# A fused attention and two-layer feed-forward kernel: w_out loaded per unit, y's first tile prepared in wider steps, attention spread evenly

## The chip, the cores and the metric

The program runs on one core of a Trainium2 chip. The metric is the device time of one execution in microseconds; less is better.

## The reference

q, k and v have the shape 4 x 8 x 576 x 64 (batch, heads, positions, columns). Per head there are two attentions: one over positions averaged in groups of four (144 x 144), whose output is repeated four times, and one over a band of seven positions around each query. Their sum, as 2304 tokens of 512 columns, goes through two feed-forward blocks:

```python
out_up = np.repeat(sm_attn(q_d, k_d, v_d), factor, axis=2)
out_local = softmax(where(abs(i - j) < 4, scale * q @ k.T, -1e9)) @ v
x = (out_up + out_local) as (2304, 512)
h = ((x @ w1) * (x @ w2)) @ w3          # 512 -> 1024 -> 1024
y = h @ w_out                           # 1024 -> 512
h2 = y @ w_in                           # 512 -> 2048
out = (h2 * sigmoid(h2)) @ w_out2       # 2048 -> 512
```

The weights arrive as 64-bit floats and are turned into pairs of 32-bit numbers on the chip. Every large matmul is made of three passes (line 31): high times high, low times high, high times low.

## The kernel before, in words

**Opening (about the first 110 us).** The weights w3 and w_out of the first block are loaded, decoded to 32 bits (`decode`, line 140: one activation on ScalarE and four instructions on VectorE, lines 164 to 176, and a split in high and low in lines 188 and 189) and multiplied with each other to one matrix WP (`wprime`, line 438), since nothing stands between them. The first attention steps run beside that.

**Slots.** Then come 192 slots, each a group of 12 matmuls: `ab_group` (line 529, x @ w1 or x @ w2 for one of eight pieces m of 128 columns) and `y_group` (line 570). A token group is a batch b and a part h of 320 or 256 tokens. Batches 0 to 2 go through h = 0 and h = 1 in turn, 16 ab slots each, and the 8 y slots of a group stand behind the first two ab slots of the next one. Batch 1 begins at slot 40, batch 2 at 88, batch 3 at 136. In batch 3 the pieces m < 4 of both parts come first; its last ab slots are 178 to 183 and its last y slots 184 to 191. The accumulators of ab and y have four PSUM buffers (tag mm). The copies `af` (line 545) and `yo` (line 587) on ScalarE and the product `cf` (line 552) on VectorE free them. `yo` has two SBUF buffers, each of which is stored to DRAM (line 589) before it is used again.

**Attention steps.** 48 steps (16 pairs of heads; `scores`, `turn`, `sums`, lines 402 to 417) are put between the slots by a pace: after slot i the steps up to n // 3 + 1 have been written, with n from line 828. `sums` makes x (`make_x`, line 378: the high half on ScalarE, line 392, and the low half on GpSimd, line 393). An ab group needs the x of its four pairs; the last x of batch 1 is made in step 25, of batch 2 in step 37, of batch 3 in step 48.

**Background work.** The weights of the second block, w_in and w_out2, are loaded, decoded and stored to DRAM in 16 units (`bg_steps`, line 632), planned for slots 14 to 166. The weights w12 for m = 4 to 7 are decoded at slots 0, 4, 7 and 10, and used from slots 8, 10, 12 and 14 on. What `at(slot, ...)` plans for a slot is written ahead of it, behind the last instructions marked on ScalarE, VectorE and GpSimd (`behind`, line 812). SP's requests are not held by that.

**Order.** The order of the instructions of each engine, up to the last stage, is set by a scheduler when the program is built: of what is ready it takes what was written first. In the last stage the order of TensorE, VectorE, ScalarE and GpSimd is that of the program (line 966). SP issues every DMA, in an order that the scheduler sets throughout, and waits for each request's buffer before it sends the next.

**First tile of y.** The last stage works on three tiles of 768 tokens. `y_load` (line 737) brings a tile from DRAM into one buffer (tag raw). From its four blocks `y_mix` (line 750, GpSimd) makes four differences t1 to t4, and `y_high` (line 759, ScalarE) and `y_rest` (line 765, GpSimd for even i, VectorE for odd i) split seven blocks into high and low. Later tiles do this inside the units; for tile 0 it is planned behind slot bg_end = 169, with all of it in slots 170 to 174 (lines 803 to 807).

**Last stage, 24 units.** `h_unit` (line 908) makes seven products (a scheme with seven instead of eight block products) of a tile with 256 columns of w_in: for each i six matmuls into one of two PSUM buffers (tag S), then sums on VectorE (line 914); the first product is copied to `p1` on ScalarE (line 932). `silu` (line 889) then makes the two halves of g: a sigmoid on ScalarE, a multiply and a rounding on VectorE (lines 896 and 897) and the low half on GpSimd (line 899); the second half's are put off to the next group by `after`. The 12 `out_block`s (line 845) of unit u, three matmuls each, run between the groups of unit u + 1, two behind each but the first. They need the piece p of w_out2 for that unit: `wo_load(p)` (line 786), 1 MB from DRAM into a buffer with the tag wA (p < 4, taken over from w12) or wC (taken over from WP). The first four are planned for slots 184 to 187, the others are written ahead of unit 0. After the last unit of a tile six outputs of 128 x 512 are copied to SBUF, into three buffers (line 862), and stored in two pieces each (line 869).

Of the kernel before, what the change touches and what calls it, by code (L numbers as in the profile page):

```python
# [8 lines left out]
F32 = mybir.dt.float32  # L9
# [26 lines left out]
def tile_model(ctx: ExitStack, tc: tile.TileContext, qk, vw, vr, w12, w3t, wo, wb, out):  # L36
    nc = tc.nc
# [28 lines left out]
    def s_tile(name):  # L66
        return ps.tile([P, 512], F32, tag="S", name=name, bufs=2)

    ident = cst.tile([P, P], F32, name="ident")
    make_identity(nc, ident)  # L70

# [642 lines left out]
    def at(slot, fn):  # L714
        plan.setdefault(slot, []).append(fn)
# [34 lines left out]
    def y_mix(t, i):  # L750
        b = Y[t]
        out_, in0, in1 = (("t1", "b12", "b11"), ("t2", "b22", "t1"),
                          ("t3", "b22", "b12"), ("t4", "t2", "b21"))[i]
        b[out_] = b["b12"] if i == 2 else yp[0].tile(
            [P, 2, NH], F32, tag=out_, name=f"{out_}_{t}"
        )
        nc.gpsimd.tensor_tensor(out=b[out_], in0=b[in0], in1=b[in1], op=ALU.subtract)
# [4 lines left out]
        nc.scalar.copy(d[:, 0], Y[t][name])  # L762
        YC[t, i] = d

    def y_rest(t, i):
        d = YC[t, i]
        e = nc.vector if i % 2 else nc.gpsimd
        e.tensor_tensor(
            out=d[:, 1], in0=Y[t][CH[i][0]], in1=d[:, 0].bitcast(F32), op=ALU.subtract
        )  # L770
# [29 lines left out]
        y_load(0)  # L800

    at(bg_end, open_y)
    for i in range(4):
        at(bg_end + 1 + i // 2, lambda i=i: y_mix(0, i))
    for i in range(7):
        at(bg_end + 1 + i // 2, lambda i=i: y_high(0, i))
        at(bg_end + 2 + i // 2, lambda i=i: y_rest(0, i))
    at(end_b + 1, lambda: wc_load(0))
    at(end_b + 2, lambda: wc_load(1))
    for p in range(4):  # L810
        at(end_a + 1 + p, lambda p=p: wo_load(p))
    def behind(fns):
        if not fns:
            return
# [6 lines left out]
    for i, slot in enumerate(slots):  # L821
        run_plan(36 + i)
        if i == 13:
            assert n_jobs[0] == len(jobs)
            cpool_b[0] = pool(s_cb, "cpool_b", "right", bufs=2)
        behind(plan.pop(i, []))
        slot()
        n = 36 + max(0, i - 3) if i < 40 else 72 + ((i - 39) * 36) // 46
        run_steps(n // 3 + 1)
        if not opened and done_steps[0] == NSTEP:  # L830
            s_att.close()
            late.append(pool(s_late, "late", "left"))
            opened = True
            assert i < starts[N_EARLY], (i, starts[N_EARLY])
# [4 lines left out]
    s_c.close()  # L839
    s_x.close()  # L840
    b2 = pool(ctx, "b2", "right", bufs=2)
    for p in range(4, 8):
        wo_load(p)

    todo = []

    def out_block(u, half, j):
        t, p = divmod(u, 8)
        if p == 0 and half == 0:
            OUT[t, j] = ps.tile(  # L850
                [P, 512], F32, tag="T" if j < 2 else "mm", name=f"o{t}_{j}",
                bufs=2 if j < 2 else 4,
            )
        acc = OUT[t, j]
        g, w = G[u, half], WO[p]
        for n, (a, b) in enumerate(PASSES):
            nc.tensor.matmul(  # L857
                acc, lhsT=g[:, a, j * P:(j + 1) * P], rhs=w[:, b, half, :],
                start=(p == 0 and half == 0 and n == 0), stop=(p == 7 and half == 1 and n == 2),
            )  # L860
        if p == 7 and half == 1:
            o = b2.tile([P, 512], F32, tag="o", name=f"os{t}_{j}", bufs=3)
            if j % 2:
                nc.vector.tensor_copy(o, acc)
            else:
                nc.scalar.copy(o, acc)
            for k in range(2):
                r0 = 64 * ORDER[(t * 2 * NH + j * P) // 64 + k]
                nc.sync.dma_start(out[r0:r0 + 64, :], o[64 * k:64 * k + 64, :])
# [19 lines left out]
    def silu(u, half, c):  # L889
        sg = temp("sg", f"{u}_{half}", 2, 2 * NH)  # L890
        nc.scalar.activation(sg, c, AF.Sigmoid)  # L891
        g = b2.tile([P, 2, 2 * NH], F32R, tag="g", name=f"g{u}_{half}", bufs=5)
        G[u, half] = g

        def rest():
            nc.vector.tensor_tensor(out=sg, in0=c, in1=sg, op=ALU.mult)
            nc.vector.tensor_copy(g[:, 0], sg)  # L897
            e = nc.vector if u == NUN - 1 else nc.gpsimd
            e.tensor_tensor(  # L899
                out=g[:, 1], in0=sg, in1=g[:, 0].bitcast(F32), op=ALU.subtract  # L900
            )

        if half == 0:
            rest()
        else:
            after(1, rest)

    def h_unit(u):
        t, p = divmod(u, 8)
        wc = WC.pop(u)  # L910
        k = {}

        def tt(out_, in0, in1, op=ALU.add):
            nc.vector.tensor_tensor(out=out_, in0=in0, in1=in1, op=op)  # L914

        cf = temp("c", f"f{u}", 2, 2 * NH)
        cg = None
        for i, (name, w, c) in enumerate(CH):
            acc_full = s_tile(f"h{u}_{i}")
            acc = acc_full[:, :NH]  # L920
            y = YC[t, i]
            n = 0
            for kt in range(2):
                for (a, b) in PASSES:
                    nc.tensor.matmul(  # L925
                        acc, lhsT=wc[w][:, a, c, kt * P:(kt + 1) * P], rhs=y[:, b, kt, :],
                        start=(n == 0), stop=(n == 5),
                    )
                    n += 1
            if i == 0:  # L930
                k["p1"] = temp("p1", u)
                nc.scalar.copy(k["p1"], acc)  # L932
            elif i == 1:
                tt(cf[:, :NH], acc, k["p1"])
            elif i == 2:
                k["u2"] = temp("u2", u)
                tt(k["u2"], acc, k["p1"])
            elif i == 3:
                k["u4"] = temp("u4", u)
                tt(k["u4"], acc, k["u2"])  # L940
            elif i == 4:
                tt(cf[:, NH:], acc, k["u4"])
            elif i == 5:
                cg = temp("c", f"g{u}", 2, 2 * NH)
                k["u3"] = temp("u3", u)
                tt(k["u3"], acc, k["u2"])
                tt(cg[:, NH:], acc, k["u4"])
            else:
                tt(cg[:, :NH], k["u3"], acc, ALU.subtract)
            next_chain()  # L950
            if i == 4:
                silu(u, 0, cf)
            elif i == 6:
                silu(u, 1, cg)
            if p == 7 and t + 1 < NT:
                after(1, lambda i=i: y_high(t + 1, i))
                after(3, lambda i=i: y_rest(t + 1, i))
            if 2 <= p < 6 and i == 5 and t + 1 < NT:
                y_mix(t + 1, p - 2)
            run_out(2 if i else 0)  # L960
        wc_load(u + 2)
        if p == 1 and t + 1 < NT:
            y_load(t + 1)
# [67 lines left out]
```

## Time and profile before

| | us |
|---|---|
| median of 3 runs | 899.86 |
| lowest and highest | 895.21, 900.3 |
| the profiled execution | 895.1 |
| its span, first to last instruction | 893.3 |
| TensorE busy in it | 852.6 |
| mean granted clock of TensorE | 0.987 |

The profile is of one execution, not of the median: durations and waits are read from it and summed against its 895.1 us. A group of rows of one kind gives busy time, the mean of one in ns, and the idle time of the engine ahead of it with what ended that. In a row of the timeline the brackets hold the idle time ahead of the instruction and its releaser.

### The profile page before, as it was taken

Reading aid. Unit: us, or ns where it says so; the run is one execution under the profiler, and the core shown is the slowest. Engines: PE = TensorE matmul, PEld = TensorE weight load, DVE = VectorE, ACT = ScalarE, POOL = GpSimd, SP = SyncE. Lnnn points to the kernel's source line nnn. Section 1 sums busy time; section 2 is a strip of 40 time slices with the busy share of each in tenths; the row PEclk is TensorE's granted clock in tenths of the full one; section 3 lists DMA queues with packets and bytes.
Section 4 is the critical chain, followed back from the end, with each engine's and each line's share of the span. In section 5 each row is a group of like instructions: output and inputs, shape, how many; then the busy total and the mean of one; then the engine's idle time right before and its main releaser. Section 6 shows DMA issues by size and latency. Waiting matters only on the chain.

```text
span 893.3 us, 17448 instructions
## 1 busy us (share of the span) xinstructions
PE 852.6 (95%) x7104; PEld 749.6 (84%) x7104; DVE 532.6 (60%) x852; ACT 300.9 (34%) x865; POOL 286.2 (32%) x224
## 2 busy tenths in 40 slices
PE   3999999998999999999999799999999999999996
PEld 2544598998999899999999788889889898888885
DVE  5999988675575857437954244435644356543434
ACT  5765556354444444433422111113111113211101
POOL 2000144354352534322328022424424236221220
PEclk9999998999999999999999999999999999999999
DMA  9935634554446463406983932424644242542403
GB/s 334 353 106 196 220 133 158 190 181 167 171 159 198 142 225 115 164 27 208 335 344 122 369 124 92 156 83 151 190 142 154 83 154 94 174 145 84 164 2 71
DMA packets 39729, 149.17 MB, mean 167 GB/s; under 512 B 4448, under 2 KB 11616, under 8 KB 33504
## 3 DMA queue, kind: packets, MB, share of 16 engines
q1 hardware_dynamic: 39648, 148.05, 48.0%
q8 instruction: 56, 0.92, 0.4%
q14 instruction: 25, 0.20, 0.1%
HBM read 115.52 MB, written 32.51 MB: 166 GB/s over the span
## 4 chain that ended last, share of the span: by engine, by line
PE 81%; DVE 8%; DMA 4%; ACT 2%; issue 2%; POOL 2%; SPq 1%; POOLq 0%; ACTq 0%; DVEq 0%
PE o L857 21%; PE ab L538 20%; PE h L925 19%; PE y L578 9%; PE wp L448 4%; PE ol L368 2%; PE tl L344 1%; PE sd L276 1%; PE s L325 1%; DMA out<-os 1%; PE od L310 1%; PE td L293 1%; DMA ydram<-yo 1%; DMA st<-w 1%; DMA yr<-ydram 1%
## 5 line engine op out<-in xcount | busy, mean ns | idle before, releaser
L857 PE MATMUL o<-wo,g 128*128 128x512 f32 x864 | 223.8, 395 | 0.0
L857 PEld LDWEIGHTS o<-wo,g 128*128 128x128 f32 x864 | 160.3, 188 | 27.2
L899 POOL TENSOR_TENSOR g<-sg,g 128x768 fp32r<-128x768 f32 x46 | 85.0, 1847 | 260.2 <-DVE g L897 244.6
L925 PE MATMUL h<-yc,wcb 128*128 128x384 f32 x576 | 118.6, 342 | 4.6 <-ACT p L932 4.6
L538 PE MATMUL ab<-x,w_wB 128*128 128x320 f32 (+1 forms) x768 | 114.3, 303 | 3.6 <-POOL x L393 2.1
L925 PEld LDWEIGHTS h<-yc,wcb 128*128 128x128 f32 x576 | 105.2, 190 | 13.7 <-ACT p L932 5.8
L538 PE MATMUL ab<-x,w_wA 128*128 128x320 f32 (+1 forms) x768 | 111.3, 302 | 1.8 <-ACT yo L587 1.8
L538 PEld LDWEIGHTS ab<-x,w_wB 128*128 128x128 f32 x768 | 106.5, 192 | 5.5 <-POOL x L393 2.6
L563 POOL TENSOR_TENSOR c<-cf,c 128x320 fp32r<-128x320 f32 (+1 forms) x64 | 73.2, 1145 | 117.9 <-DVE c L562 109.3
L578 PE MATMUL y<-c,w_wC 128*128 128x320 f32 (+1 forms) x768 | 109.7, 298 | 0.0
L538 PEld LDWEIGHTS ab<-x,w_wA 128*128 128x128 f32 x768 | 105.2, 192 | 3.2 <-ACT yo L587 2.0
L578 PEld LDWEIGHTS y<-c,w_wC 128*128 128x128 f32 x768 | 103.2, 188 | 1.3 <-issue 1.0
L925 PE MATMUL h<-yc,wca 128*128 128x384 f32 x432 | 83.6, 337 | 1.9 <-DVE cg L914 1.9
L891 ACT ACTIVATE sg<-cf 128x768 f32<-128x768 f32 x24 | 20.3, 847 | 184.4 <-DVE cf L914 184.4
L925 PEld LDWEIGHTS h<-yc,wca 128*128 128x128 f32 x432 | 76.8, 188 | 6.2 <-DVE cg L914 2.3
L448 PE MATMUL wp<-w_wo,w_w 128*128 128x512 f32 x128 | 61.3, 622 | 2.6 <-DVE w_w L176 2.6
L552 DVE TENSOR_TENSOR cf<-ab,af 128x320 f32<-128x320 f32 (+1 forms) x64 | 28.9, 452 | 55.5 <-PE ab L538 48.1
L235 POOL TENSOR_TENSOR vr<-vr 72x512 f32<-72x512 f32 x12 | 20.4, 1701 | 102.7 <-PE od L310 84.3
L891 ACT ACTIVATE sg<-cg 128x768 f32<-128x768 f32 x24 | 20.3, 847 | 90.0 <-DVE cg L914 90.0
L914 DVE TENSOR_TENSOR u<-h,u 128x384 f32<-128x384 f32 x48 | 26.6, 554 | 39.8 <-PE h L925 39.6
L249 ACT ACTIVATE band<-band,sm 128x38 f32<-128x38 f32 x144 | 44.9, 315 | 7.2 <-DVE sm L245 6.0
L448 PEld LDWEIGHTS wp<-w_wo,w_w 128*128 128x128 f32 x128 | 23.8, 197 | 27.9 <-issue 23.9
(116 smaller groups left out, 1067.8 us busy)
## 6 DMA issues: line engine op xcount, KB each, us to landing
wcb<-wsd SPq DMA_DIRECT2D x24, 1024.0 KB
wca<-wsd SPq DMA_DIRECT2D x24, 768.0 KB
sw<-wb SPq DMA_DIRECT2D x32, 512.0 KB
qk<-qk SPq DMA_DIRECT2D x16, 579.0 KB
wsd<-res SPq DMA_DIRECT2D x8, 1024.0 KB
wod<-res SPq DMA_DIRECT2D x8, 1024.0 KB
wo<-wod SPq DMA_DIRECT2D x8, 1024.0 KB
st<-w SPq DMA_DIRECT2D x14, 512.0 KB
```

Source lines behind the costliest of these rows:

```text
L235: side().tensor_tensor(out=r[:, :, 0:2, :], in0=r[:, :, 0:2, :], in1=r[:, :, 2:4, :], op=ALU.add)
L249: nc.scalar.activation(E[:, j, :], src[:, j, :], AF.Exp, bias=nb[:, j:j + 1], scale=scale, accum_out=sv[:, j:j + 1],)
L448: nc.tensor.matmul(acc, lhsT=w3v[:, k, j * P:(j + 1) * P], rhs=wov[:, k, :], start=(gp == 0 and k == 0), stop=(gp == 3 and k == 1),)
L538: nc.tensor.matmul(acc[:, :N], lhsT=wv[:, i, w, kk, :], rhs=x[:, j, :], start=(n == 0), stop=(n == 11),)
L552: nc.vector.tensor_tensor(out=cf, in0=acc[:, :N], in1=C.pop("af"), op=ALU.mult)
L563: mark(nc.gpsimd.tensor_tensor(out=c[:, 1], in0=cf, in1=c[:, 0].bitcast(F32), op=ALU.subtract))
L578: nc.tensor.matmul(acc[:, :N], lhsT=WP[kf // 2][:, i, kf % 2, ec * P:(ec + 1) * P], rhs=c[:, j, :], start=(kf == 0 and n == 0), stop=(kf = ...
L857: nc.tensor.matmul(acc, lhsT=g[:, a, j * P:(j + 1) * P], rhs=w[:, b, half, :], start=(p == 0 and half == 0 and n == 0), stop=(p == 7 and h ...
L891: nc.scalar.activation(sg, c, AF.Sigmoid)
L899: e.tensor_tensor(out=g[:, 1], in0=sg, in1=g[:, 0].bitcast(F32), op=ALU.subtract)
L914: nc.vector.tensor_tensor(out=out_, in0=in0, in1=in1, op=op)
L925: nc.tensor.matmul(acc, lhsT=wc[w][:, a, c, kt * P:(kt + 1) * P], rhs=y[:, b, kt, :], start=(n == 0), stop=(n == 5),)
```

## The change

A table load is forced at the start by a small activation. In `y_rest` the rests of tile 0 all go to VectorE. The differences of tile 0 are planned for slots 170, 173, 176 and 179, the seven conversions for slots 170 to 181 and each rest one slot behind its conversion. The pace reaches n = 72 at slot 37 instead of 39, and its end at slot 129 instead of 128. `wo_load(0)` is written ahead of unit 0 and `wo_load(u + 1)` at the begin of unit u. The six outputs of the last tile go into one tile of the size and tag of the y buffer. In unit 0 the multiply and rounding of the first half of g are put off by two groups.

```diff
@@ -66,6 +66,9 @@
     def s_tile(name):
         return ps.tile([P, 512], F32, tag="S", name=name, bufs=2)
 
+    early = cst.tile([P, 2], F32, name="early")
+    nc.vector.memset(early, 0.0)
+    nc.scalar.activation(early[:, 1:2], early[:, 0:1], AF.Abs)
     ident = cst.tile([P, P], F32, name="ident")
     make_identity(nc, ident)
 
@@ -762,9 +765,9 @@
         nc.scalar.copy(d[:, 0], Y[t][name])
         YC[t, i] = d
 
-    def y_rest(t, i):
+    def y_rest(t, i, alone=False):
         d = YC[t, i]
-        e = nc.vector if i % 2 else nc.gpsimd
+        e = nc.vector if i % 2 or alone else nc.gpsimd
         e.tensor_tensor(
             out=d[:, 1], in0=Y[t][CH[i][0]], in1=d[:, 0].bitcast(F32), op=ALU.subtract
         )
@@ -800,15 +803,13 @@
         y_load(0)
 
     at(bg_end, open_y)
-    for i in range(4):
-        at(bg_end + 1 + i // 2, lambda i=i: y_mix(0, i))
-    for i in range(7):
-        at(bg_end + 1 + i // 2, lambda i=i: y_high(0, i))
-        at(bg_end + 2 + i // 2, lambda i=i: y_rest(0, i))
+    for i, k in enumerate((1, 4, 7, 10)):
+        at(bg_end + k, lambda i=i: y_mix(0, i))
+    for i, k in ((0, 1), (1, 2), (3, 3), (2, 6), (4, 7), (5, 9), (6, 12)):
+        at(bg_end + k, lambda i=i: y_high(0, i))
+        at(bg_end + k + 1, lambda i=i: y_rest(0, i, True))
     at(end_b + 1, lambda: wc_load(0))
     at(end_b + 2, lambda: wc_load(1))
-    for p in range(4):
-        at(end_a + 1 + p, lambda p=p: wo_load(p))
     def behind(fns):
         if not fns:
             return
@@ -825,7 +826,7 @@
             cpool_b[0] = pool(s_cb, "cpool_b", "right", bufs=2)
         behind(plan.pop(i, []))
         slot()
-        n = 36 + max(0, i - 3) if i < 40 else 72 + ((i - 39) * 36) // 46
+        n = 36 + (i * 36) // 37 if i < 37 else 72 + ((i - 37) * 3) // 4
         run_steps(n // 3 + 1)
         if not opened and done_steps[0] == NSTEP:
             s_att.close()
@@ -839,10 +840,11 @@
     s_c.close()
     s_x.close()
     b2 = pool(ctx, "b2", "right", bufs=2)
-    for p in range(4, 8):
-        wo_load(p)
+    wo_load(0)
 
     todo = []
+
+    last = []
 
     def out_block(u, half, j):
         t, p = divmod(u, 8)
@@ -859,7 +861,12 @@
                 start=(p == 0 and half == 0 and n == 0), stop=(p == 7 and half == 1 and n == 2),
             )
         if p == 7 and half == 1:
-            o = b2.tile([P, 512], F32, tag="o", name=f"os{t}_{j}", bufs=3)
+            if t < NT - 1:
+                o = b2.tile([P, 512], F32, tag="o", name=f"os{t}_{j}", bufs=3)
+            else:
+                if not last:
+                    last.append(yp[0].tile([P, 6, 512], F32, tag="raw", name="last"))
+                o = last[0][:, j]
             if j % 2:
                 nc.vector.tensor_copy(o, acc)
             else:
@@ -900,15 +907,17 @@
                 out=g[:, 1], in0=sg, in1=g[:, 0].bitcast(F32), op=ALU.subtract
             )
 
-        if half == 0:
+        if half == 0 and u:
             rest()
         else:
-            after(1, rest)
+            after(2 - half, rest)
 
     def h_unit(u):
         t, p = divmod(u, 8)
         wc = WC.pop(u)
         k = {}
+        if u < 7:
+            wo_load(u + 1)
 
         def tt(out_, in0, in1, op=ALU.add):
             nc.vector.tensor_tensor(out=out_, in0=in0, in1=in1, op=op)
```

## Rows read from the trace of the kernel before

**Rows 1.** The page: busy time, share of the span and instructions of each engine.

```profile
PE 852.6 (95%) x7104; PEld 749.6 (84%) x7104; DVE 532.6 (60%) x852; ACT 300.9 (34%) x865; POOL 286.2 (32%) x224
```

**Rows 2.** TensorE's waits: line waited for, us in total, times, longest.

```profile
PE h L925 <- ACT p L932: 4.6, 3, 3.4
...
PE ab L538 <- POOL x L393: 2.1, 2, 1.6
PE h L925 <- DVE cg L914: 1.9, 1, 1.9
PE ab L538 <- ACT yo L587: 1.8, 1, 1.8
```

**Rows 3.** Windows: busy us of PE, PEld, DVE, ACT, POOL; PEclk, DMA share, GB/s.

```profile
125.00:150.00 25.00, 23.82 (x364) 20.92 (x361) 23.59 (x37) 12.53 (x41) 13.87 (x11) 0.93 0.55 182
145.00:153.00 8.00, 8.00 (x98) 7.37 (x95) 7.90 (x12) 3.17 (x9) 5.91 (x4) 0.58 0.77 248
204.00:212.00 8.00, 5.30 (x25) 4.77 (x24) 3.39 (x8) 1.82 (x4) 3.78 (x5) 0.79 0.77 274
478.00:486.00 8.00, 6.16 (x39) 5.96 (x38) 4.90 (x5) 2.54 (x6) 8.00 (x5) 0.79 0.12 18
500.00:510.00 10.00, 6.55 (x29) 6.41 (x29) 2.23 (x4) 1.93 (x4) 0.00 (x0) 0.83 0.92 359
510.00:516.00 6.00, 4.06 (x22) 3.51 (x21) 4.90 (x8) 1.34 (x3) 2.22 (x2) 1.00 0.82 300
```

**Rows 4.** Timeline of the opening: start us, us, engine, line, operation.

```profile
8.21 1.28 ACT L164 ACT_TABLE_LOAD   x1 [8.21 <-DMA lent<-wo]
...
10.69 0.69 DVE L165 TENSOR_SCALAR w_wo<-w_wo 128x1024 f32<-128x1024 f32 x1 [0.22 <-ACT w_wo L164]
```

**Rows 5.** Timeline at slot 40, the first of batch 1.

```profile
205.61 0.56 PE L538 MATMUL ab<-x,w_wB 128*128 128x320 f32 x2 [1.08 <-ACT x L392]
...
206.17 2.26 POOL L393 TENSOR_TENSOR x<-xf,x 128x320 fp32r<-128x320 f32 x2
```

**Rows 6.** VectorE and TensorE near slot 10 (timeline); pooling on VectorE (groups).

```profile
128.78 1.69 DVE L189 TENSOR_TENSOR w_wA<-dec,w_wA 128x1024 fp32r<-128x1024 f32 x1 [0.35 <-ACT w_wA L188]
...
130.46 3.79 PE L538 MATMUL ab<-x,w_wA 128*128 128x320 f32 x24
...
L229 DVE TENSOR_REDUCE qkd<-qk 128x288 f32<-128x1152 f32 x10 | 13.4, 1340 | 0.0
```

**Rows 7.** The chain that ended last, 460 to 530 us: start us, us, what.

```profile
470.57 2.57 POOL t L757
...
480.16 0.43 ACT yo L587
...
480.63 6.05 PE ab L538 x36
...
494.20 8.12 DMA ydram<-yo
```

**Rows 8.** Rests of y on VectorE: ns min, median, max; first and last start.

```profile
L768 DVE TENSOR_TENSOR yc<-yr,yc x6: 948/1846/2425, 469.5 to 755.6; 128x768 fp32r<-128x768 f32 x6
```

**Rows 9.** Timeline of SP's requests, 425 to 530 us.

```profile
460.49 0.32 SPq L788 DMA_DIRECT2D wo<-wod  x1
...
483.74 0.37 SPq L741 DMA_DIRECT2D yr<-ydram  x1
...
484.75 2.27 SPq L788 DMA_DIRECT2D wo<-wod  x3
```

**Rows 10.** Timeline of VectorE and GpSimd in unit 0.

```profile
510.05 0.96 DVE L896 TENSOR_TENSOR sg<-cf,sg 128x768 f32<-128x768 f32 x1 [0.92 <-ACT sg L891]
...
511.68 1.82 POOL L899 TENSOR_TENSOR g<-sg,g 128x768 fp32r<-128x768 f32 x1 [23.24 <-DVE g L897]
```

**Rows 11.** The end: SP's last stores (timeline), and one's landing (chain).

```profile
883.00 7.51 SPq L869 DMA_DIRECT2D out<-os  x12
...
886.08 2.40 DMA out<-os
```

## The prediction

> **What bounds the kernel now.** I read the page first: TensorE is busy 852.6 of 893.3 us [rows 1], so a change that leaves the matmuls alone can only win back TensorE's idle time and the time that it runs at the lower clock. So next came the list of TensorE's waits: apart from the opening, where it waits for its first data, four kinds remain that the change can touch: for the x of a new batch, for the copy yo, for the copy p and for the sum cg [rows 2]. Then the windows around them, with the granted clock, because a wait costs more than itself. The two levels are 1.0 (2.4 GHz) and 0.5 (1.2 GHz), so (1 - clock) times the stretch is what the lower level took. From 204 to 212 us: 8 - 5.30 = 2.7 idle and 0.21 x 8 = 1.7 at the lower level, together 4.4. From 478 to 486: 1.84 + 1.7 = 3.5. From 500 to 510: 3.45 + 1.7 = 5.1. From 510 to 516: 1.94 idle, the clock full. From 145 to 153 TensorE never idles, but the clock is 0.58: 3.4 lost between small attention matmuls [rows 3]. The later units hold only the two smaller waits for p, 4.6 - 3.4 = 1.2 [rows 2], and nothing in the change shortens a matmul. So some 14 us of waits and their clock are there to be won, and the opening, where VectorE is full, is where something can be lost.
>
> The profiled execution took 895.1 us, its span 893.3. I make the sum against 895.1; the three timed runs are 895.21, 899.86 and 900.3, of which it equals the fastest.
>
> **Early table load.** The load takes 1.28 us on ScalarE, after the first weights have landed [rows 4]. The new first activation does it while ScalarE has nothing else. But VectorE waited only 0.22 us for that activation [rows 4], being busy with the sums of v until then. I take 0.2 us; the ends are 0 and 1.28. The Trainium skill (ScalarE: Activation LUTs, "What ACT_TABLE_LOAD costs") counts a drain with each load and comes to 2.66 us; the row shows 1.28 and the activation right behind it, and by the page's figure the upper end alone would grow, to 2.66.
>
> **Pace of attention.** Slot 40 is the first that needs all x of batch 1; the last of them comes from attention step 25, which n = 72 allows. Before, n is 72 at slot 39, directly ahead of slot 40; after, at slot 37. TensorE waited there first for x's high half, then for the low half on GpSimd [rows 5]. Two slots more are 24 matmuls: 3.79 us for those with 320 columns [rows 6], four fifths of it, 3.0, with 256 as here. The same distance stands already at batch 2 (n = 108 at slot 85 in both versions, needed at slot 88), and there the wait for x is the smaller of the two: 2.1 - 1.6 = 0.5 [rows 2]. So I expect 0.5 idle to stay and the clock to hold: 4.4 - 0.5 = 3.9 won. If the clock falls all the same, it is 2.2.
>
> The price is in the opening. From slot 4 on each step comes two slots sooner, so one step more is done before slot 14, which needs the last early weights. VectorE is busy 23.6 of 25 us from 125 to 150 [rows 3], and weights are just in time: the low half of w12's m = 5 is written from 128.78 for 1.69 us, to 130.47, and TensorE's next group begins at 130.46 [rows 6]. The added step is a turn; its main VectorE instruction, the pooling of q and k, takes 1.34 us [rows 6], with its small copy 1.65 by estimate. What it holds up is the next decode, and behind that the matmuls of slots 12 to 14. Below I bound the loss by nothing (TensorE's own share of the step fills the wait) or a gain of 3.4 (the low-clock stretch of 145 to 153 goes, since the small matmuls fall elsewhere); above by two late decodes, each 1.65 and a clock loss of 1.7, 6.7 in all. I take a loss of 1.2, nearest the one pooling. The later slots run at a slightly slower pace and end one slot later, at 129, where the last batch needs its x only at slot 136: nothing.
>
> **First tile of y at wider steps.** Before, four subtractions on GpSimd, three conversions behind them on ScalarE and the rests were queued within five slots. ScalarE waited for each subtraction in turn, and the copy yo, which frees the accumulator that TensorE needs next, came only at 480.16; TensorE went on at 480.63 [rows 7]. After, a conversion follows its subtraction by two slots or more, and yo is queued ahead of the last ones. All seven rests go to VectorE, which is idle for most of this stretch; GpSimd keeps only the subtractions, at most 4 x 2.57 = 10.3 us [rows 7], from 468 on, done by about 479. Nobody needs t4 before the seventh group of unit 0, 20 us later. The wait goes: 3.5 won. What is late next is yo's store, below. If the subtractions were later than I think, the wait would return; the ends are 0 and 3.5.
>
> A rule of the Trainium skill speaks against this part: GpSimd shares its SBUF interfaces with VectorE, with contention where VectorE reads two SBUF inputs (GPSIMD Engine Reference, "8. Key points"). The trace agrees: VectorE's rests range from 0.95 to 2.43 us with a median of 1.85 [rows 8]. By the rule alone the whole tile takes longer than on two engines kept apart. By the rows seven rests at 1.85 are 13 us, inside the 25 us before unit 0, and the sum stays.
>
> **w_out per unit.** At 494.2 a store of yo goes out and takes 8.12 us to land [rows 7], behind y of tile 1 and three to five pieces of w_out of 1 MB each [rows 9]. The next yo copy waits for that buffer, and the copy p of unit 0 behind it in ScalarE's queue holds TensorE 3.4 us [rows 2]. If each piece goes out at its unit, only piece 0 and y are in front of the store, and the wait goes with its clock loss: 5.1 won. But the place in the program does not fix when SP sends it: the four pieces written for after the last ab slot begin at 460.49, while the ab matmuls still run at 480.63 [rows 7, 9]. Requests go out as their buffers come free, so pieces 1 to 7 may still leave ahead of unit 0. Even then the bunch should be looser: three pieces left together at 484.75 only because SP stood waiting to refill y, until 483.74 [rows 9], and that buffer is now free about 5 us sooner. So I take 5.1; the ends are 0 and 5.1. Pieces needed: piece p by unit p + 1's second group, a whole unit after the request. SP stands waiting for freed wc buffers in between; that can use up a part of the unit and leaves the landing inside it.
>
> **Delayed product in unit 0.** Before, the multiply (0.96), the rounding (with hand-over 0.67, up to 511.68) and three adds stood on VectorE in this order [rows 10], and TensorE waited 1.94 for the adds [rows 3]. After, the adds come first. But the first out blocks of unit 1 need the product's low half, and GpSimd takes 1.82 for it [rows 10]. By estimate, a group of h is 1.1 (3.79 / 24 [rows 6], x 384 / 320 columns, x 6 matmuls), an add 0.5 (half the columns of the multiply), and the sigmoid ahead of it 0.9. Counted from the end of cf, before and at full clock: 0.9 + 0.96 + 0.67 and two adds, 3.5, until the accumulator is free, two groups, first out block at 5.7. After: the adds end at 2.2 behind groups 5 and 6, the low half is done at 2.2 + 0.96 + 0.67 + 1.82 = 5.7, while TensorE stands ready at 3.6. So the wait moves from h to o; 0.2 is what I take for it, and the ends are -1.7 (the clock falls at the new wait) and 1.9.
>
> **Six output buffers.** Before, copies waited for buffers, yet SP sent the twelve stores without a gap: 7.51 us for 12 [rows 11], 0.6 each, from the moment the first copy was done. More buffers do not change SP's pace. I take 0.2; the ends are 0 and 0.5.
>
> **The sum.** 0.2 + 3.9 - 1.2 + 3.5 + 5.1 + 0.2 + 0.2 = 11.9, so 895.1 - 11.9 = 883.2. Two of three runs stood 4.7 us higher than the profiled one, for a reason that no trace here shows. I put the median in the middle: 883.2 + 2.4, about 886.
>
> **Rivals**, each with the same 2.4.
> - The loading of w_out does not do what it says: the pieces leave as before and yo's store waits behind them. For it: 460.49 against 480.63 [rows 7, 9]. Against: the bunch at 484.75 had a cause that goes. It gives 883.2 + 5.1 = 888.3, with the 2.4 about 891.
> - VectorE's opening takes the gain: 6.7 instead of 1.2. For it: 23.6 of 25 us, weights just in time [rows 3, 6]. Against: one step of 1.65 is all that moves ahead of slot 14. It gives 888.7, about 891.
> - The opening gains: no loss, and the 3.4 of 145 to 153 goes: 878.6, about 881.
> - Slower than before: the six outputs share one tile, and if the tile is tracked as a whole, each copy waits for the store of the one before to land. Per copy 0.6, two stores of 0.6 and a landing of 2.4 [rows 11], 4.2 in all; six are 25, where the span now ends 10.3 after the first store, at 883.0 [rows 11]. That is 15 more: 898.2, about 901. It decides the sign once a cycle exceeds (10.3 + 11.9) / 6 = 3.7 us. Against: TensorE reads the high half of an x tile from 205.61, though the low half, which the program writes ahead of every read, starts on GpSimd only at 206.17, so parts of a tile are tracked singly [rows 5].
>
> **How the numbers follow.** The forecast 0.50, w_out as before 0.22, the opening's loss 0.15, its gain 0.09, the whole-tile end 0.04. The range is 878 (the opening's gain without the 2.4) to 896 (the first two rivals together, 893.8 + 2.4). About 1%, 9 us, is what a measurement can tell from no change, so faster means below 890.9: of the forecast nine in ten, of each of the first two rivals half, and the opening's gain, some 0.72. Slower is the last rival and what I have not thought of: 0.05. The rest, 0.23, is within 1%.
>
> **What would show it.** Right: no wait for x over 0.6 us and full clock after the last slot of batch 0; no wait for yo ahead of the last ab slots; first h groups of unit 0 back to back; a new wait of o for GpSimd's product in unit 1, 1 to 2 us; SP's twelve last stores still 7 to 7.5 us; the table load alone near 1 us. Wrong: a yo store over 5 us and a wait of h for p (w_out), TensorE idle between 115 and 155 us over 2.5 (opening), last stores over 10 us (whole tile).

## The result, and the profile after

| | us |
|---|---|
| kernel before, median of 4 runs | 898.3 (895.21 to 900.3) |
| changed kernel, median of 4 runs | 885.33 (884.52 to 886.44) |
| ratio, 95% interval | 0.986 (0.982 to 0.990) |
| profiled execution of the changed kernel; its span | 884.5; 882.7 |

Faster by 1.4%, and 0.7 us from the forecast of 886.0. The steps behind that number did far worse than the number. The first signs are in the profile. The page, against [rows 1]: TensorE works 6.5 us less for the same 7104 matmuls. The lower clock explains little of it (its mean is 0.987 before and 0.988 after, some 1 us of the span); the rest was in no step of the prediction.

```profile
PE 846.1 (96%) x7104; PEld 745.7 (84%) x7104; DVE 533.8 (60%) x857; ACT 300.5 (34%) x866; POOL 277.5 (31%) x220
```

TensorE's waits, against [rows 2]. The waits for x, for yo and for cg are gone. The wait of h for p has grown (longest 3.4, now 4.2), and o waits for GpSimd's low half.

```profile
PE h L934 <- ACT p L941: 5.8, 3, 4.2
...
PE o L859 <- POOL g L906: 2.0, 1, 2.0
```

Windows of the same places as [rows 3], moved with the work (columns as there). Batch 1's first slot and the last ab slots run without a gap at full clock; from 145 to 155 the clock is still low (0.66), and 488 to 502, unit 0, is worse than before: 4.2 us idle and a clock of 0.76.

```profile
125.00:150.00 25.00, 23.36 (x364) 20.61 (x364) 24.43 (x37) 12.11 (x37) 14.44 (x11) 0.96 0.49 156
145.00:155.00 10.00, 9.82 (x153) 9.33 (x153) 8.43 (x16) 3.45 (x10) 4.04 (x4) 0.66 0.57 196
200.00:208.00 8.00, 8.00 (x107) 7.92 (x100) 6.78 (x11) 3.73 (x13) 6.40 (x6) 1.00 0.27 67
468.00:476.00 8.00, 8.00 (x70) 8.00 (x69) 7.84 (x8) 4.38 (x8) 5.50 (x3) 1.00 0.15 41
488.00:502.00 14.00, 9.82 (x42) 9.29 (x40) 3.13 (x6) 1.97 (x4) 0.00 (x0) 0.76 0.87 340
502.00:509.00 7.00, 4.96 (x25) 4.28 (x25) 5.47 (x7) 1.33 (x2) 4.21 (x2) 1.00 0.74 265
```

Unit 0 on TensorE (timeline), then SP's requests around it, which answer to [rows 9]. The 24 matmuls behind the wait take 6.89 us (4.33 at full clock, below), so the wait and the clock behind it cost 4.18 + 2.56 = 6.7 us.

```profile
487.74 2.25 PE L934 MATMUL h<-yc,wca 128*128 128x384 f32 x12
494.16 6.89 PE L934 MATMUL h<-yc,wcb 128*128 128x384 f32 x24 [4.18 <-ACT p L941]
```

```profile
484.10 0.32 SPq L592 DMA_DIRECT2D ydram<-yo  x1
484.86 0.32 SPq L791 DMA_DIRECT2D wo<-wod  x1
485.51 5.74 SPq L592 DMA_DIRECT2D ydram<-yo  x2
491.34 0.38 SPq L791 DMA_DIRECT2D wo<-wod  x1
493.75 0.32 SPq L592 DMA_DIRECT2D ydram<-yo  x1
494.17 0.89 SPq L791 DMA_DIRECT2D wo<-wod  x2
```

All eight pieces of w_out (the first at 454.07) are still requested by 495.1 us, when unit 0 has only begun its third group, and now one stands between the first and the second store of yo and one between the third and the fourth. The chain that ended last shows what that does: the second store takes 7.75 us, and the copies yo and p wait behind it.

```profile
485.51 7.75 DMA ydram<-yo
...
493.36 0.04 ACT yo L590
493.40 0.23 issue
493.63 0.49 ACT p L941
```

The end and the start: SP's twelve last stores take 7.53 us (7.51 in [rows 11]); the table load now stands alone at 0.74 us and takes the same 1.28.

```profile
0.74 1.28 ACT L71 ACT_TABLE_LOAD   x1 [0.74 <-PEq L1030]
...
872.43 7.53 SPq L876 DMA_DIRECT2D out<-last  x12
```

### The profile page after: what moved, and what is told of

Its sections match the earlier page's. It is cut to its first block, busy times and chain, and to the rows that moved or that the text cites. A ratio compares the mean times of both kernels' runs of the same rounds, so it can differ in the third digit from the quotient of the medians.

```text
span 882.7 us, 17438 instructions
## 1 busy us (share of the span) xinstructions
PE 846.1 (96%) x7104; PEld 745.7 (84%) x7104; DVE 533.8 (60%) x857; ACT 300.5 (34%) x866; POOL 277.5 (31%) x220
## 4 chain that ended last, share of the span: by engine, by line
PE 83%; DVE 8%; DMA 3%; ACT 2%; issue 2%; SPq 0%; POOL 0%; ACTq 0%; DVEq 0%
PE o L859 21%; PE ab L541 20%; PE h L934 19%; PE y L581 10%; PE wp L451 5%; PE ol L371 2%; PE sd L279 2%; DMA ydram<-yo 2%; PE tl L347 2%; PE s L328 1%; PE od L313 1%; DMA out<-os 1%; PE td L296 1%; DVE dec L175 1%; DMA lent<-wo 1%
## 5 line engine op out<-in xcount | busy, mean ns | idle before, releaser
L541 PE MATMUL ab<-x,w_wB 128*128 128x320 f32 (+1 forms) x768 | 111.0, 299 | 0.6 <-DVE cf L555 0.6
L541 PE MATMUL ab<-x,w_wA 128*128 128x320 f32 (+1 forms) x768 | 108.9, 299 | 0.6 <-DVE w_wA L192 0.6
L541 PEld LDWEIGHTS ab<-x,w_wB 128*128 128x128 f32 x768 | 103.8, 190 | 2.1 <-issue 1.0
```

What stands on the lines that cost most here:

```text
L541: nc.tensor.matmul(acc[:, :N], lhsT=wv[:, i, w, kk, :], rhs=x[:, j, :], start=(n == 0), stop=(n == 11),)
```

## The experiments

Two things had to be explained: the 5.1 us for w_out that did not come, and TensorE's faster matmuls that nobody had ordered. The first four kernels each undo one part. The experiments ran beside the kernel before (medians of 898.1, 897.1 and 897.9 in three sets of runs); I set their medians against the changed kernel's 885.33. The intervals reach 2 to 4 us to either side, so a difference of that size between two medians needs the traces beside it.

**w_out as it was loaded before.**

```diff
+    for p in range(4):
+        at(end_a + 1 + p, lambda p=p: wo_load(p))
...
-    wo_load(0)
+    for p in range(4, 8):
+        wo_load(p)
...
-        if u < 7:
-            wo_load(u + 1)
```

> The changed kernel, with the loads of w_out written where they stood before (four pieces behind the last slots of ab, four behind the loop). Theory: the place in the program never decided when SP sends a piece; the scheduler had spread them among the stores of yo in both versions, so the new place won nothing. Then this kernel takes what the changed kernel takes, within 1.5 us (ratio to the kernel before 0.984 to 0.989), and unit 0 still waits 3.4 to 4.2 us for p. Rival: one piece per unit did win its 5.1 us, and something else lost it again in unit 0. Then this kernel is 4 to 6 us slower than the changed one (ratio 0.991 or more) and the wait for p grows beyond 4.2 us.

Measured 881.9 (881.38 to 884.65), ratio 0.984 (0.981 to 0.988): 3.4 us faster than the changed kernel. Both theories fall. The new place was not worth nothing, it cost something. The medians alone would not show that, since their intervals overlap; SP's timeline and TensorE's in this kernel do:

```profile
483.10 1.74 SPq L592 DMA_DIRECT2D ydram<-yo  x2
484.94 0.39 SPq L791 DMA_DIRECT2D wo<-wod  x1
490.86 0.79 SPq L592 DMA_DIRECT2D ydram<-yo  x2
```

```profile
491.63 4.43 PE L935 MATMUL h<-yc,wcb 128*128 128x384 f32 x24 [2.64 <-ACT p L942]
```

The stores go in pairs with a piece behind each pair, the wait is 2.64 instead of 4.18 and the clock holds (4.43 instead of 6.89): 4.0 us in unit 0. Other executions bear it out: from unit 0's first matmul to unit 1's, this kernel takes 10.4 us, and the five kernels with w_out at its new place, two buffers for yo, the new tile of y and the delayed product take 13.7 to 14.4.

**The old pace.**

```diff
-        n = 36 + (i * 36) // 37 if i < 37 else 72 + ((i - 37) * 3) // 4
+        n = 36 + max(0, i - 3) if i < 40 else 72 + ((i - 39) * 36) // 46
```

> The changed kernel with the attention's old pace. Theory: the even pace won 3.9 us at slot 40 and 1.8 us more where batch 2 begins, and cost under 1 us in the opening. Then the waits for x come back (2 to 4 us idle at the first slots of batches 1 and 2, the clock falls behind them), batch 1's y starts about 4 us and batch 3's about 6 us later than in the changed kernel, and the whole takes 4 to 6.5 us more (ratio 0.991 to 0.994). Rival: the opening pays for it, and slots 0 to 14 run faster by 2 us or more with the old pace; then the whole is only 1 to 3 us slower than the changed kernel.

Measured 889.14, ratio 0.992 (0.989 to 0.994): 3.8 us slower, just under the expected span. At slot 40 both waits are back:

```profile
207.80 0.56 PE L541 MATMUL ab<-x,w_wB 128*128 128x320 f32 x2 [1.16 <-ACT x L395]
209.99 2.17 PE L541 MATMUL ab<-x,w_wB 128*128 128x320 f32 x13 [1.63 <-POOL x L396]
```

Behind these waits the clock held here (1.00 from 204 to 216 us), as it did in another kernel with the old pace (the tile alone, below); the fall to 0.79 [rows 3] was of the one execution. The rival falls: the opening doesn't pay for the new pace. It doesn't clearly gain either. From the first ab matmul to the first y matmul (both in TensorE's timeline) the three kernels of the old pace take 46.0, 47.4 and 48.4 us, the eleven of the new one 43.4 to 46.6, median 45.0. But the stretch doesn't hold the same work: at the old pace 530 or 542 matmuls stand in it, at the new one 500 (498 in one kernel); the difference, all of it attention, now stands behind the first y matmul. Two kernels that ran it at full clock show what is left, first the tile alone with the old pace, then four buffers for yo with the new one (both below; columns as in [rows 3]; PEld counts a weight load for each matmul):

```profile
111.08:157.08 46.00, 43.64 (x530) 40.00 (x531) 42.71 (x67) 28.05 (x95) 22.49 (x17) 1.00 0.45 146
111.41:154.93 43.52, 41.86 (x509) 38.49 (x501) 40.08 (x64) 25.26 (x83) 21.62 (x18) 1.00 0.47 149
```

The 216 ab matmuls among them keep TensorE busy for 33.6 and 33.4 us, the idle time is 2.4 and 1.7: a gain of 0.7. In the other two kernels of the old pace the idle time is 1.2 (the kernel before) and 3.3 (this one), in the changed kernel 1.7, so the opening's part is not to be told from nothing. Some 3 us of the eleven's spread is the clock alone. The changed kernel and the one with four buffers for yo (below) have the same TensorE order there and equal busy time, but from 145 to 155 us the clock of the first is 0.66 (above) and that of the second full:

```profile
145.00:155.00 10.00, 9.82 (x176) 9.36 (x176) 9.64 (x19) 6.23 (x26) 4.26 (x5) 1.00 0.58 193
```

**The first tile of y at the old steps, on the old engines.** The lines of the diff at `y_mix`, `y_high` and `y_rest` taken back.

> The changed kernel with the first tile of y prepared at the old steps on the old engines. Theory: the wait for yo ahead of the last ab slots (1.8 us and the lower clock behind it) comes back and costs 3.5 us, up to 3.7: ratio 0.989 to 0.991. Rival: with the even pace the stretch is looser and the wait stays away; then nothing changes, or the wait is only passed on to unit 0's wait for p, which shrinks by as much (ratio 0.985 to 0.987).

Measured 887.71, ratio 0.989 (0.986 to 0.992): 2.4 us slower. The wait for yo is back, and the later start hands a longer wait on to unit 0:

```profile
475.34 4.35 PE L541 MATMUL ab<-x,w_wA 128*128 128x256 f32 x36 [1.86 <-ACT yo L590]
...
498.71 3.57 PE L934 MATMUL h<-yc,wcb 128*128 128x384 f32 x10 [6.05 <-ACT p L941]
```

From the first y matmul of batch 2's second part to unit 0, this kernel takes 87.8 us and the changed one 84.7.

**Without the early table load.**

```diff
-    early = cst.tile([P, 2], F32, name="early")
-    nc.vector.memset(early, 0.0)
-    nc.scalar.activation(early[:, 1:2], early[:, 0:1], AF.Abs)
```

> The changed kernel without the first, empty activation. Theory: the early load of the table did not help; by taking VectorE's and ScalarE's first place it made the scheduler order the early work in another way, and the first ab slot began 1.1 us later than in the kernel before. Without it that slot begins 1.1 us sooner, at 110.3 us, and the whole is about 1 us shorter (ratio 0.984 to 0.986). Rival: the 1.1 us come from another part or from the chip; then the first ab slot stays at 111.4 us or moves back by the 0.2 to 1.3 us of the load, and the whole grows by as much.

Measured 888.53 (883.65 to 889.82), ratio 0.990 (0.986 to 0.993): not shorter but 3.2 us longer by the medians, while the first ab slot begins at 112.6 us, not sooner than the changed kernel's 111.4. The theory falls. Up to that slot the order on all four engines is that of the kernel before, where it began at 110.3, so its start moves by 2 us between executions of one order and tells nothing of the load. The rival's reason is not it either, since the loss is not in the opening: the first y matmul comes at 156.7 us, in the changed kernel at 158.0. It is in every unit. The copy p of two ordinary units in a row gives the time of one: 15.78 us here as in the kernel before, 15.66 in the changed kernel. (First the kernel before, then the changed kernel, then this one.)

```profile
783.92 0.48 ACT L932 COPY p<-h 128x384 f32<-128x384 f32 x1 [1.02 <-PE h L925]
...
799.70 0.48 ACT L932 COPY p<-h 128x384 f32<-128x384 f32 x1 [1.02 <-PE h L925]
```

```profile
789.82 0.48 ACT L941 COPY p<-h 128x384 f32<-128x384 f32 x1 [1.00 <-PE h L934]
...
805.48 0.48 ACT L941 COPY p<-h 128x384 f32<-128x384 f32 x1 [1.00 <-PE h L934]
```

```profile
808.91 0.48 ACT L938 COPY p<-h 128x384 f32<-128x384 f32 x1 [1.02 <-PE h L931]
...
824.69 0.48 ACT L938 COPY p<-h 128x384 f32<-128x384 f32 x1 [1.02 <-PE h L931]
```

What has a table load at 0.74 us to do with a unit at 800? It brought a tile. `early` is the first tile of the left side of SBUF; its 8 bytes a partition are rounded to 32, and the attention's tiles, the weights, the tiles of y and w_out lie 32 bytes higher, while x, c and g on the right side stay. The next two kernels take the tile and the load apart.

**The tile alone, in the kernel before.**

```diff
+    early = cst.tile([P, 2], F32, name="early")
+    nc.vector.memset(early, 0.0)
     ident = cst.tile([P, P], F32, name="ident")
```

> The kernel before with nothing but the tile early (8 bytes a partition, 32 with padding) and its memset, no activation and no other part of the change. The order of instructions on TensorE stays; every tile of the left side of SBUF, the weights among them, lies 32 bytes higher, those of the right side stay. Theory: where the tiles lie sets how fast TensorE reads its two operands; with the 32 bytes a unit takes 15.66 us in place of 15.78, in 22 units 2.6 us, with some of the ab stage about 3 us, ratio 0.996 to 0.998. Rival: the units' 15.66 us belong to the early load or to the rest of the change; then a unit stays at 15.78 us and the ratio is 0.999 to 1.001.

Measured 890.43, ratio 0.992 (0.989 to 0.995): 4.8 to 9.9 us from eight bytes. TensorE's order is that of the kernel before, but for one pair of neighbours. A unit takes 15.66:

```profile
827.05 0.48 ACT L934 COPY p<-h 128x384 f32<-128x384 f32 x1 [1.00 <-PE h L927]
...
842.71 0.48 ACT L934 COPY p<-h 128x384 f32<-128x384 f32 x1 [1.00 <-PE h L927]
```

**The load alone, without the move.**

```diff
-    early = cst.tile([P, 2], F32, name="early")
+    early = att.tile([P, 2], F32, tag="early", name="early", bufs=1)
```

> The changed kernel with the tile early taken from the attention's pool, which is closed before y is opened: the early activation stays, but the weights and the tiles of y lie where they lay in the kernel before. Theory of the places: a unit takes 15.78 us again and the whole 3 us more than the changed kernel, ratio 0.988 to 0.991. Rival (the load or the order of the work that comes with it): a unit takes 15.66 us, ratio 0.985 to 0.987.

Measured 888.10, ratio 0.989 (0.987 to 0.992), and a unit takes 838.80 - 823.02 = 15.78:

```profile
823.02 0.48 ACT L941 COPY p<-h 128x384 f32<-128x384 f32 x1 [1.02 <-PE h L934]
...
838.80 0.48 ACT L941 COPY p<-h 128x384 f32<-128x384 f32 x1 [1.02 <-PE h L934]
```

The order on all four engines is that of the changed kernel. (Of the attention's own tiles, those behind `early` still lie 32 bytes higher here; the weights, y and w_out don't.) So the 15.66 belong to where the tiles lie and not to the load, whose own worth is the 0.4 us between this kernel and the one without it: not to be told from nothing.

**w_out really held back.** Each piece is put behind a request of SP with an order edge (`issue_after`): pieces 0 and 1 behind the last store of yo, piece u + 1 behind the weights that unit u - 1 requests (`wc_load` keeps its last request in `spq` too).

```diff
-            nc.sync.dma_start(ydram[ec, :, t0:t0 + N], yo)
+            spq[0] = nc.sync.dma_start(ydram[ec, :, t0:t0 + N], yo)
...
+        with tc.issue_after(spq[0].ins):
+            nc.sync.dma_start(t.rearrange("p l f n -> p (l f n)").bitcast(F32), wod[p])
```

> The changed kernel with every piece of w_out put behind the last store of yo on SP's queue, and piece u+1 behind the weights of unit u. Theory: the stores of yo then have no piece of 1 MB in front of them, take 2 to 3 us each and not 5, the copies yo and p come at once, TensorE's wait for p in unit 0 falls from 4.2 us to under 1 us and the clock stays up behind it: 5 to 6.5 us off the changed kernel, 879 to 880 us, ratio 0.978 to 0.981. Rival: the load of y's second half of tile 1 or the weights of unit 1 in the same queues hold the stores as much; then the wait for p stays above 2.5 us and the gain is under 2 us. A second one: piece 0 or 1 lands too late for its unit, and TensorE waits for it at the first out blocks.

Measured 878.46, ratio 0.978 (0.975 to 0.981): 6.9 us off the changed kernel, a little more than expected. The four stores go out in one run with the pieces behind them, and unit 0 runs without a wait for p, at full clock:

```profile
484.11 4.61 SPq L593 DMA_DIRECT2D ydram<-yo  x4
488.83 1.12 SPq L795 DMA_DIRECT2D wo<-wod  x2
```

```profile
487.75 2.25 PE L938 MATMUL h<-yc,wca 128*128 128x384 f32 x12
489.84 4.33 PE L938 MATMUL h<-yc,wcb 128*128 128x384 f32 x24
```

Neither rival shows. The idea of one piece per unit was worth what I had put on it and more; the edit did not carry it out.

**Four buffers for yo.**

```diff
-            yo = cpool.tile([P, TOK[0]], F32, tag="yo", name=f"yo{b}_{h}_{ec}")[:, :N]
+            yo = cpool.tile([P, TOK[0]], F32, tag="yo", name=f"yo{b}_{h}_{ec}", bufs=4)[:, :N]
```

> The changed kernel with four buffers for yo in place of two, w_out left as it is. Theory: what holds ScalarE's copy p is only that the copy yo ahead of it waits for a buffer; with four buffers no copy yo waits, unit 0's wait for p goes (4.2 us and 2.4 us of the lower clock), 5 to 6.5 us off, 879 to 880 us, though the stores land as late as before. Rival: the last copies are held by something else, the accumulators or SP; then the wait stays above 2.5 us.

Measured 876.3, ratio 0.977 (0.974 to 0.980): 9.0 us off, more than the 6.7 of that wait. (The clock of the opening, above, explains some 3 us of its profile, 873.6, but not surely of its median.) A piece still stands between the first and the second store here (481.24 us), and the copies no longer wait for the stores: the second 24-matmul run begins at once, 486.21 behind 484.13. So the same wait goes from either end: give the stores a free queue, or give the copies a free buffer.

**Four buffers, and the low half of unit 0's first product on VectorE.**

```diff
-            e = nc.vector if u == NUN - 1 else nc.gpsimd
+            e = nc.vector if u == NUN - 1 or u + half == 0 else nc.gpsimd
```

> The changed kernel with four buffers for yo, and the low half of unit 0's first product on VectorE in place of GpSimd. Theory: the wait of 1.97 us for GpSimd at unit 1's first out block goes, as VectorE is done with that half in about 1 us; 1 to 2 us off the kernel with four buffers alone (876.3 us), 874.5 to 875.5 us, ratio 0.974 to 0.977. Rival: VectorE's extra instruction holds up the sums of unit 1's first groups, and the wait moves from o to h: no gain, 876 us and a wait of h for a sum of over 1 us.

Measured 874.03 (872.49 to 875.67), ratio 0.974 (0.971 to 0.976): the fastest kernel of this study, 2.6% below the kernel before and 2.3 us below the last. The trace shows 1.5 of these: the wait of 1.97 us falls to 0.44.

```profile
496.26 1.43 PE L859 MATMUL o<-wo,g 128*128 128x512 f32 x5 [0.44 <-DVE g L906]
```

**The same, 64 bytes higher in place of 32.**

```diff
-    early = cst.tile([P, 2], F32, name="early")
+    early = cst.tile([P, 16], F32, name="early")
```

> The same kernel with a tile early of 64 bytes a partition in place of 8, so that the left side of SBUF lies 64 bytes higher than in the kernel before, and not 32. TensorE's order is the same. Theory A: what counts is the distance of the two operands in steps of 32 bytes, odd or even; then 64 bytes are as 0 bytes, a unit takes 15.78 us and the whole 3 to 5 us more than with 32. Theory B: any distance other than that of the kernel before is better; then a unit takes 15.66 us and the whole the same as with 32.

Measured 881.71, ratio 0.983 (0.980 to 0.985): 7.7 us slower than with 32 bytes, with the same order on all four engines. The traces show 6.6 of it: 24 x 0.18 = 4.3 in the units and 2.3 in the slots (297.4 against 295.1 us from the first y matmul of batch 0 to that of batch 3). A unit takes 835.87 - 820.03 = 15.84 us:

```profile
820.03 0.48 ACT L941 COPY p<-h 128x384 f32<-128x384 f32 x1 [1.02 <-PE h L934]
...
835.87 0.48 ACT L941 COPY p<-h 128x384 f32<-128x384 f32 x1 [1.02 <-PE h L934]
```

Theory B falls. Theory A has the side right and not the size: 64 bytes are not as 0, they are a little worse. The timelines also say which matmuls it is. In a unit the 42 of h, from each one's start to the next matmul's, take 7.39 us at 0 bytes, 7.36 at 32 and 7.44 at 64, the 36 of o 8.39, 8.30 and 8.40. The first twelve of h show it, from their start to that of o: 2.10, 2.08 and 2.11 us (the kernel before, the changed kernel, this one).

```profile
814.17 2.26 PE L925 MATMUL h<-yc,wca 128*128 128x384 f32 x12
816.27 1.56 PE L857 MATMUL o<-wo,g 128*128 128x512 f32 x6
```

```profile
804.18 2.25 PE L934 MATMUL h<-yc,wca 128*128 128x384 f32 x12
806.26 1.54 PE L859 MATMUL o<-wo,g 128*128 128x512 f32 x6
```

```profile
802.87 2.27 PE L934 MATMUL h<-yc,wca 128*128 128x384 f32 x12
804.98 1.56 PE L859 MATMUL o<-wo,g 128*128 128x512 f32 x6
```

Both operands of h (the weights and y) lie on the left and moved together. So the distance between the two operands of a matmul, on which theory A rests, can't be the whole reason.

**Unit 0's product at once, and three buffers for the last tile.** The conditions in `silu` and in `out_block` taken back, one in each kernel.

> The changed kernel with the product of unit 0's first half in its old place, ahead of the adds. Theory: the delay only moved a wait: the wait of o for GpSimd (1.97 us) goes, the wait of h for the sum cg (1.9 us) comes back, and the time stays within 1 us of the changed kernel, ratio 0.984 to 0.987. Rival: the delay won the 1.9 us whole; then this one is 2 us or more slower, with both waits in its list.

> The changed kernel with three buffers for the last tile's outputs. Theory: the last matmul to the end of the span stays at 7.5 us, since SP's twelve requests of 0.6 us set it; within 0.5 us of the changed kernel, ratio 0.984 to 0.987. Rival: the buffers did win something; then that stretch grows to 8 us or more.

Measured 883.98, ratio 0.984 (0.980 to 0.989), and 883.47, ratio 0.984 (0.981 to 0.987): neither part can be told from nothing. In the first, h waits 2.0 us for cg again and no o waits for GpSimd: the delay had only moved the wait.

```profile
PE h L934 <- DVE cg L923: 2.0, 1, 2.0
```

In the second SP sends its last twelve stores in the same time:

```profile
871.23 7.52 SPq L871 DMA_DIRECT2D out<-os  x12
```

## Why the prediction was right, and where it was wrong

The number was right because misses cancelled. Found by medians is the difference to 885.33 when the part is undone; found by traces is the part's own stretch.

| term | forecast | found by medians | found by traces |
|---|---|---|---|
| w_out per unit | +5.1 (0 to 5.1) | -3.4 | -3.2 to -4.0 |
| pace, slot 40 and opening | +3.9 - 1.2 = +2.7 | +3.8 | +4.5, most of it the waits at slot 40 |
| first tile of y | +3.5 | +2.4 | +3.1 |
| early table load | +0.2 | +0.4 | not separable |
| product of unit 0 | +0.2 | -1.4 | a wait moved, 1.97 for 2.0 |
| six output buffers | +0.2 | -1.9 | 7.53 for 7.52 |
| place of the left side of SBUF | not in the sum | +2.8, or 6.7 added alone | +5: units 24 x 0.12 = 2.9, ab slots 2 |

The place is read, in the slots, from the first y matmul of batch 0 to that of batch 3: 295.1 to 297.1 us, median 295.7, in the seven kernels that have the left side 32 bytes higher, the new pace and the new tile of y; 297.9 and 298.1 in the two that have the new pace and the left side where it was. The pace is read from the first ab matmul to the first y matmul of batch 3, which holds the same work at either pace: 344.6 and 345.7 us in the two with the old pace and the left side 32 bytes higher, 338.6 to 342.5, median 340.7, in the same seven. TensorE idles for 7.1 and 7.8 us of it with the old pace and for 2.8 to 4.7 in the seven; between the first y matmuls of batch 0 and batch 1, where slot 40 lies, for 3.5 and 2.8 against 0.0 to 1.0.

By the traces the parts make 8.6 to 9.4 (the moved wait and the stores at nothing), where the profiled executions lie 10.6 apart and the medians 13.0 (9.4 to 15.8 by the interval). In the profiles 1.7 us more are the lower clock at slot 40 of the kernel before. The rest I can't place; the clock of the opening moves by 3 us between executions of one order, and the start of the first ab slot by 2.

- **w_out: the step failed, past its own lower bound.** I named the mechanism, that the place in the program does not fix when SP sends, and made it a rival at 0.22. What failed is the sentence "Even then the bunch should be looser", and with it 0 as the worst end. I thought of requests that leave as their buffers come free. SP's order is fixed when the program is built; moving the text changed where that order puts a piece of 1 MB among four stores of 128 KB, and it put one between the first and the second. The sign I had written down, a yo store over 5 us and h waiting for p, is what the profile showed (7.75 and 4.18).
- **Pace: right about slot 40's waits, too dark about the opening.** In the changed kernel no wait for x is left, not even the 0.5 I had kept, and the clock held. The idle time is worth 2.8 to 3.5 us there; the 1.7 for the clock came out in one execution of the old pace and not in the other two. In the opening I took a loss of 1.2 nearest to one pooling of 1.34 us; found is 0.7 us less idle time at full clock, with 1.2 to 3.3 us of idle time among the kernels of the old pace: nothing that can be told. The third rival, at 0.09, fails too: from 145 to 155 us the clock is 0.66 in the changed kernel and 1.00 in the tile alone with the old pace. That stretch follows the execution and not the pace.
- **First tile of y: right**, mechanism and size.
- **Unit 0: the product right.** The wait moved from h to o, 1.97 us by GpSimd as forecast. "First h groups of unit 0 back to back" was wrong, because of w_out.
- **Table load, six buffers: right**, near nothing. That one tile would serve six copies without whole-tile waits is right too.
- **Missing altogether:** the tile `early` itself. That "nothing in the change shortens a matmul" was wrong: I priced its activation and not its 8 bytes, and they are worth as much as any other part. With w_out at its measured -4.0 and nothing else changed, my sum would have given 886.0 + 9.1, some 895.
- **"Two of three runs stood 4.7 us higher than the profiled one, for a reason that no trace here shows":** in 35 more runs the kernel before lies between 893.8 and 901.0, with medians of 897.1 to 898.1, so its profile was of a run at the lower end, and adding half of the difference was right.
- **A small slip:** the four places with waits add up to 4.4 + 3.5 + 5.1 + 1.9 = 14.9 us, not to "some 14"; no term hangs on it.

## What to carry to other kernels

Where a load is written says little about when it is sent: read the queue's own order in both versions, ask what large request stands ahead of each small store that frees a buffer, and fix the order with an edge or make the wait harmless with one more buffer. When every matmul of a kernel gets faster or slower by a part of a per cent, look at where its operands lie before looking for a cause in the work. And undo each part alone, even when the total is right: two errors of several us were hidden in a forecast that missed by 0.7.

## What the hardware showed that I had not expected

The same TensorE order takes 15.66 or 15.84 us a unit (and in its other variants 15.78) by whether the left side of SBUF lies 32 or 64 bytes (or 0) higher, while the right side stays; whole kernels differ by 7.7 us (874.03 and 881.71), of which the traces show 6.6. The clock was full in those units (1.00 from 780 to 850 us), so it isn't the clock. The Trainium skill (SBUF — State Buffer, "Operand start alignment") asks only that an operand start at a multiple of its element size, and says that this is about legality and not speed. All three places here are such multiples, so by the rule alone there is nothing to choose between them; the runs show that there is. Both h, with its two operands on the left, and o, with one on each side, changed. What in the place makes the difference, and with what period, was not tried: weights, y and w_out moved together in every run.
